# First weight pair of a spectral-mix kernel: rows of 8192 bytes, four modes per transfer and per product

## The chip, the cores and the metric

The kernel runs on one core of a Trainium2 chip. The metric is device time in microseconds (us) of one execution, all input and output transfers included. The core has TensorE (PE in the profile; PEld is its weight load), VectorE (DVE), ScalarE (ACT), GpSimd (POOL) and SyncE (SP), which here issues nearly all transfers. SBUF is the on-chip memory of 128 partitions, PSUM the memory that TensorE writes to. An engine works through its own instructions in order and waits on semaphores for the others.

## What is computed

Two stages, cut to what matters here. First, sliding-window attention with a distance bias, 8 batches, 8 heads, 576 positions, head size 64:

```python
scores = scale * np.matmul(q, k.transpose(0, 1, 3, 2))
mask = (rel >= 0) & (rel < 128)
scores = np.where(mask, scores + bias[None], -1000000000.0)
attn = softmax(scores)                       # over the last axis
x = np.matmul(attn, v)                       # -> (8, 576, 512) after the heads are joined
```

Then a mix in the spectrum along the positions, with complex weights of 512 x 512 for each of the lowest 64 modes, and a last product:

```python
X = np.fft.rfft(x, axis=1)                   # Xr, Xi: first 64 modes
Yr = np.einsum('bmd,mde->bme', Xr, w_r) - np.einsum('bmd,mde->bme', Xi, w_i)
Yi = np.einsum('bmd,mde->bme', Xr, w_i) + np.einsum('bmd,mde->bme', Xi, w_r)
y = np.fft.irfft(Y, n=S, axis=1)
u = x + y
return u + np.maximum(u @ w_ch, 0.0)
```

w_r and w_i are float32, 64 x 512 x 512 each: 134 MB together, most of what the kernel reads.

## The kernel before

**Units and pairs.** Two heads make a pair, whose outputs are 128 of the 512 columns d of x. GROUPS = ((0,), (1, 2, 3)) puts pair 0 into a first group and the other three into a second. A unit is one pair of one batch: 8 units of the first group, then 24 of the second, N = 32 in all.

**Slots.** The program is ordered by hand. `_slot(n)` writes out one step of a pipeline over the units, in this order: the first scores of unit n (PE) with their exponential (ACT, L450) and mask product (DVE, L455); the transposes of q and k of unit n+1 (PE, L411) with their copies out of PSUM (ACT, L419); the items of w0, which are products with weights; the second scores and their exponential; the casts of q, k and v to bf16 on POOL (L388, L400); the spectrum of unit n-2 (L530); the product with v of unit n-1 (L484); the mask product L460; the items of w1. An engine takes its share of this in the order written.

**Spectrum.** `_spectrum` multiplies x by a table F of cosines and sines and leaves real and imaginary part of 64 modes for the 128 columns d on 128 partitions. For the first group four batches share one PSUM tile `xt`; two DVE instructions (L540, L541) write the tile X[0], which holds -imaginary, real and imaginary part side by side. For the second group a DVE copy (L536) writes Xn, and X is made later, for eight modes at a time, by `_select`.

**Why `_select` is there.** A transfer of the second group takes, for two modes, rows of six consecutive d (12288 bytes), which puts 64 partitions of one mode and 64 of the other alternately on the 128 partitions. One product then sums over both modes' d at once, and its other operand must hold the right mode's values on each partition and zeros on the others. `_select` makes that operand on PE with selector matrices `sel`, built once by `_sel_rows` from the identity, and copies the result from PSUM with DVE (real and imaginary part) and ACT (the negative).

**Weights.** A ring of 12288 float32 per partition holds weights that wait for use. `g.parts` lists the loads: for the first group 64 parts of two modes of w_r or w_i (1024 values per partition, two rows of 2048 bytes), then 64 parts of the second (3072 values). `_load_w` issues the next part on SP as soon as the program has passed the products that use the room it needs; it is called after each `_modes`. The twelve first parts are issued among the loads of q, k and v at the start. SP's loads use eight semaphores in turn, so that each waits for the one eight before it.

**Products of the first group.** `_modes(g, 0, m0, w)` multiplies the part's weights (the upper halves of the float32 values, read as bf16) with X: for each of four blocks of 128 output columns and each of two modes a weight load and a product of 16 columns (two components x eight batches), summed in a PSUM tile `acc` for eight modes, which ACT copies to ZTa at the end. An item is two modes, w_r and w_i: 16 products. The 32 items are spread over slots 10 to 35 by the list `steps`, about one a slot and about 1.6 from slot 24 on.

**Second group.** After slot 35 the products of the second group follow with their selects, together with the work of the output as far as it is known; then `_finish`.

Of the kernel before, what the change touches and what calls it, by code (L numbers as in the profile page):

```python
# [9 lines left out]
FP32 = mybir.dt.float32  # L10
BF16 = mybir.dt.bfloat16
# [5 lines left out]
P = 128  # L17
MB = 8
# [3 lines left out]
ROWS = (1, 6)  # L22
SIZE = (1024, 3072)
# [19 lines left out]
def kernel(  # L43
# [26 lines left out]
    g.parts = [(j, m, w) for j in range(len(GROUPS)) for m in range(0, NM, 2) for w in range(2)]  # L70
# [13 lines left out]
    g.Xn = persist.tile([P, len(GROUPS[-1]), 2, B, NM], BF16)  # L84
    g.sel = persist.tile([P, 2, 2, P], BF16)
# [8 lines left out]
    with tc.manual_schedule(engines={ET.SP, ET.PE, ET.Activation, ET.DVE, ET.Pool}):  # L94
        with ExitStack() as wctx:
# [5 lines left out]
            with ExitStack() as actx:  # L101
                cp = actx.enter_context(tc.tile_pool(name="const", bufs=1))
                for j, grp in enumerate(GROUPS[:-1]):
                    g.X[j] = cp.tile([P, ROWS[j], 3, B, NM], BF16, name=f"X{j}")
# [15 lines left out]
                for n in range(n0):  # L120
                    _load_unit(g, n)
                    if n < VB - 1:
                        _load_v(g, n)
                    elif n >= VB + 2:
                        _load_v(g, n - 3)
                    if n >= g.first[1] - 1:
                        for _ in range(2):
                            _load_w(g)
# [26 lines left out]
                for j in range(len(GROUPS) - 1):  # L155
                    steps = []
                    for n in range(g.first[j + 1] + 2, g.first[j + 2] + 2):
                        steps += [n] * (SHARE if n < N - LA else SHARE_END)
                    if j + 2 == len(GROUPS):
                        steps += [n for n in range(N + 2, N + 2 + TAIL)] * SHARE_END  # L160
                    steps.sort()
                    for i, m in enumerate(range(0, NM, 2)):
                        work[steps[i * len(steps) // (NM // 2)]].append((j, m))
                _sel_rows(g)
# [25 lines left out]
            _select(g, 0)  # L190
            rest_w = [(m, w) for m in range(0, NM, 2) for w in range(2)]
            with ExitStack() as xctx:
# [4 lines left out]
                while k < len(g.seq):  # L197
# [3 lines left out]
                    if done % MB == 5 and done + 3 < NM:  # L201
                        _select(g, done + 3)
# [304 lines left out]
def _spectrum(g, n):  # L507
# [25 lines left out]
    if b % nb == nb - 1:  # L533
        b0 = b - nb + 1
        if j:
            nc.vector.tensor_copy(g.Xn[:, :, :, b], xt[:, 0])  # L536
            return
        X = g.X[j]
        xi = xt[:, :, 0].rearrange("p b i m -> p i b m")
        nc.vector.tensor_copy(X[:, 0, 1:3, b0 : b0 + nb], xi)  # L540
        nc.vector.tensor_scalar_mul(X[:, 0, 0, b0 : b0 + nb], xi[:, 1], -1.0)  # L541


def _sel_rows(g):

    nc = g.nc
    nc.vector.memset(g.sel, 0.0)
    for o in range(2):
        for h in range(2):
            nc.vector.tensor_copy(g.sel[:, o, h, h::2], g.ident_b[:, o::2])  # L550


def _select(g, m0):


    nc = g.nc
    A = len(GROUPS[-1])
    X = g.zp.tile([P, 2 * A, 3, MB, g.B], BF16, tag="Xz", bufs=2, name="Xz")
    for o in range(2):
        ps = g.fps.tile([P, g.DM], FP32, tag=("mm", "y")[o], name="xz")  # L560
        ps = ps[:, 0 : A * 2 * MB * g.B].rearrange("p (c i m b) -> p c i m b", i=2, m=MB, b=g.B)
        for h in range(2):
            nc.tensor.matmul(
                ps.rearrange("p c i m b -> p (c i) m b")[:, :, h::2], lhsT=g.sel[:, o, h],
                rhs=g.Xn.rearrange("p c i b m -> p (c i) m b")[:, :, m0 + h : m0 + MB : 2],
                start=True, stop=True)
        r = slice(A * o, A * o + A)
        nc.vector.tensor_copy(X[:, r, 1:3], ps)  # L568
        nc.scalar.mul(X[:, r, 0], ps[:, :, 1], -1.0)  # L569
    g.X[len(GROUPS) - 1, m0 // MB] = X  # L570


def _slot(g, n, w0, w1):


    N = len(g.units)
    if n < N:
        _score(g, n, 0)
# [33 lines left out]
def _places(parts):  # L612


    size = SIZE
    n0 = sum(1 for p in parts if p[0] == 0)
    at = (-n0 * size[0]) % RING
    out = []
    for j, _, _ in parts:
        if at + size[j] > RING:  # L620
            at = 0
        out.append((at, at + size[j]))
        at = (at + size[j]) % RING
    return out


def _load_w(g):
# [11 lines left out]
    src = (g.w_r, g.w_i)[w][m0 : m0 + 2, r0 : r0 + len(GROUPS[j]) * P]  # L639
# [18 lines left out]
def _pair_of_modes(g, j, m0):  # L658
    for w in range(2):
        _modes(g, j, m0, w)  # L660


def _modes(g, j, m0, w, last=False):
# [3 lines left out]
    X = g.X[j] if j == 0 else g.X[j, m0 // MB]  # L667
    A = ROWS[j]
# [7 lines left out]
    n = 2 // (SIZE[j] // (512 * A))  # L676
    for et in range(4):
        for a in range(SIZE[j] // 512):
            d, m = (a, m0) if n == 2 else (0, m0 + a)
            if j == 0:  # L680
                x = X[:, d, 1 - w : 3 - w, :, m]
            else:
                x = X[:, d, 1 - w : 3 - w, m % MB : m % MB + n]
            nc.tensor.matmul(  # L684
                acc[:, et, :, m - c0 : m - c0 + n, :],
                lhsT=wt[:, a, et * P : (et + 1) * P], rhs=x,
                start=(m0 == c0 and w == et == a == 0),
                stop=(m0 + 2 in ends and w == 1 and et == 3 and a == SIZE[j] // 512 - 1))
# [3 lines left out]
    m = m0 + 1  # L692
# [232 lines left out]
```

## Time and profile before

The time is 455.19 us, the median of three runs (452.93 to 455.75).

| | us |
|---|---|
| profiled execution, its own time | 455.69 |
| its span, first to last instruction | 453.9 |
| PE busy | 314.2 |
| DVE busy | 218.1 |
| ACT busy | 190.2 |
| POOL busy | 152.5 |
| bytes moved | 173.85 MB, 383 GB/s over the span |
| granted clock of TensorE, mean | 0.733 |

The profile is of one execution. A matmul's duration in it is longer than its share of PE, since matmuls are pipelined: where the rate matters, the distance of the starts is read. A row of a group gives, after the bar, busy time in us, mean of one in ns, and the idle time ahead of it with what ended it. A row of the chain of waits or of the timeline begins with the start and the duration in us. The share of the DMA engines can pass 1, since packets of one engine overlap.

### The profile page before, as it was taken

Reading aid. Unit: us, or ns where it says so; the run is one execution under the profiler, and the core shown is the slowest. Engines: PE = TensorE matmul, PEld = TensorE weight load, DVE = VectorE, ACT = ScalarE, POOL = GpSimd, SP = SyncE. Lnnn points to the kernel's source line nnn. Section 1 sums busy time; section 2 is a strip of 40 time slices with the busy share of each in tenths; the row PEclk is TensorE's granted clock in tenths of the full one; section 3 lists DMA queues with packets and bytes.
Section 4 is the critical chain, followed back from the end, with each engine's and each line's share of the span. In section 5 each row is a group of like instructions: output and inputs, shape, how many; then the busy total and the mean of one; then the engine's idle time right before and its main releaser. Section 6 shows DMA issues by size and latency. Waiting matters only on the chain.

```text
span 453.9 us, 12869 instructions
## 1 busy us (share of the span) xinstructions
PE 314.2 (69%) x5490; PEld 216.0 (48%) x5511; DVE 218.1 (48%) x428; ACT 190.2 (42%) x294; POOL 152.5 (34%) x262
## 2 busy tenths in 40 slices
PE   2677989988899984315656655656556766778993
PEld 2465677766778763213333333333333433554562
DVE  8468566648655451102442343434434433633683
ACT  4887666668755621001232322223222213322773
POOL 6799789779966402020000000000000000003564
PEclk9999555579755555556685786888676568998998
DMA  8999999999999999999999999999999999992687
GB/s 240 340 346 308 390 341 384 391 393 385 386 374 395 405 408 430 426 428 430 429 426 428 430 427 429 425 432 428 427 431 427 429 428 429 428 386 81 241 309 248
DMA packets 59465, 173.85 MB, mean 383 GB/s; under 512 B 4880, under 2 KB 21264, under 8 KB 51216
## 3 DMA queue, kind: packets, MB, share of 16 engines
q1 hardware_dynamic: 59024, 171.99, 96.4%
q0 software_dynamic: 384, 1.05, 1.0%
q8 instruction: 43, 0.70, 0.6%
q14 instruction: 14, 0.11, 0.1%
HBM read 163.58 MB, written 9.44 MB: 381 GB/s over the span
## 4 chain that ended last, share of the span: by engine, by line
DMA 45%; PE 34%; ACT 7%; DVE 6%; issue 4%; POOL 2%; POOLq 0%; ACTq 0%; DVEq 0%
DMA ring<-in_moe_w_r_dram 36%; DMA ring<-in_moe_w_i_dram 9%; PE acc L684 6%; PE sc L438 6%; PE xt L530 4%; PE tqk L411 4%; PE av L484 4%; ACT att L450 3%; ACT qkT L419 2%; PE mm L821 2%; PE mm L724 2%; PE y L821 1%; PE xw L737 1%; PE y L724 1%; DVE hl L743 1%
## 5 line engine op out<-in xcount | busy, mean ns | idle before, releaser
L684 PEld LDWEIGHTS <-ring 128*128 128x128 bf16 x2048 | 62.7, 103 | 122.7 <-DMA ring<-in_moe_w_i_dram 59.2
L684 PE MATMUL acc<-Xz,ring 128*128 128x32 bf16 x1536 | 51.2, 183 | 90.5 <-DMA ring<-in_moe_w_i_dram 46.1
L742 ACT CAST hl<-xw 64x512 bf16<-64x512 f32 x72 | 41.8, 580 | 125.9 <-PE xw L737 94.9
L450 ACT ACTIVATE att<-sc 128x1024 bf16<-128x1024 f32 x64 | 65.6, 1025 | 42.4 <-PE sc L438 30.5
L743 DVE TENSOR_TENSOR hl<-xw,hl 64x512 bf16<-64x512 f32 x72 | 49.6, 689 | 65.9 <-ACT hl L742 65.4
L400 POOL CAST vb<-v 64x256 bf16<-64x256 f32 x128 | 66.0, 516 | 20.7 <-PE av L484 12.8
L763 POOL MEMSET ZTa<- 32x512 bf16 x1 | 0.5, 515 | 189.2 <-ACT ZTa L760 189.2
L737 PE MATMUL xw<-wch,xT 128*128 128x512 bf16 x133 | 51.8, 524 | 3.8 <-issue 3.3
L438 PE MATMUL sc<-qkT,qkT 64*64 64x256 bf16 (+1 forms) x512 | 36.3, 365 | 19.8 <-ACT qkT L419 11.8
L419 ACT COPY qkT<-tqk 128x576 bf16<-128x576 bf16 x64 | 40.5, 634 | 0.9 <-PE tqk L411 0.9
L411 PE MATMUL tqk<-ident_b,qkb 64*64 64x64 bf16 x1152 | 35.3, 227 | 7.4 <-POOL qkb L388 7.0
L411 PEld LDWEIGHTS <-qkb 64*64 64x64 bf16 x1152 | 34.9, 142 | 10.4 <-POOL qkb L388 9.4
L484 PE MATMUL av<-vb,att 128*128 128x65 bf16 (+1 forms) x512 | 35.0, 231 | 0.9 <-DVE x L501 0.5
L455 DVE TENSOR_TENSOR att<-att,mask 128x1024 bf16<-128x1024 bf16 x32 | 28.2, 883 | 8.3 <-ACT att L450 8.2
L484 PEld LDWEIGHTS <-att 128*128 128x128 bf16 (+1 forms) x512 | 28.0, 122 | 7.6 <-issue 1.4
L717 DVE COPY xT<-tp 128x512 bf16<-128x512 bf16 x36 | 15.2, 422 | 30.3 <-PE tp L715 29.9
L737 PEld LDWEIGHTS <-xT 128*128 128x128 bf16 x144 | 17.7, 129 | 19.4 <-issue 16.1
L388 POOL CAST qkb<-q 128x576 bf16<-128x576 f32 x32 | 25.4, 793 | 4.2 <-DMA q<-in_q_dram 1.1
L388 POOL CAST qkb<-k 128x576 bf16<-128x576 f32 x32 | 26.0, 811 | 0.6 <-DMA k<-in_k_dram 0.5
L438 PEld LDWEIGHTS <-qkT 64*64 64x64 bf16 x512 | 13.4, 129 | 24.4 <-ACT qkT L419 14.2
L460 DVE TENSOR_TENSOR att<-att,mask 128x1024 bf16<-128x1024 bf16 x32 | 24.0, 749 | 1.5 <-ACT att L450 1.1
L569 ACT ACTIVATE Xz<-xz 128x192 bf16<-128x192 f32 x16 | 5.3, 331 | 41.2 <-DVE Xz L568 40.9
(110 smaller groups left out, 434.3 us busy)
## 6 DMA issues: line engine op xcount, KB each, us to landing
ring<-in_moe_w_r_dram SPq DMA_DIRECT2D x32, 1536.0 KB, 13.7
ring<-in_moe_w_i_dram SPq DMA_DIRECT2D x32, 1536.0 KB, 13.7
ring<-in_moe_w_r_dram SPq DMA_DIRECT2D x32, 512.0 KB, 7.0
ring<-in_moe_w_i_dram SPq DMA_DIRECT2D x32, 512.0 KB, 7.5
q<-in_q_dram SPq DMA_DIRECT2D x32, 288.0 KB, 6.5
k<-in_k_dram SPq DMA_DIRECT2D x32, 288.0 KB, 6.2
v<-in_v_dram SPq DMA_DIRECT2D x64, 128.0 KB, 5.8
out_dram<-o SPq DMA_DIRECT2D x32, 256.0 KB, 2.7
```

The costliest lines, as they stand in the source:

```text
L388: g.nc.gpsimd.tensor_copy(tb, t)
L400: g.nc.gpsimd.tensor_copy(o[64 * r : 64 * r + 64, i], v[64 * i : 64 * i + 64, r])
L411: g.nc.tensor.transpose(tp[hs, r, :], u.b[w][hs, r], g.ident_b[hs, hs], tile_position=(64 * hh, 64 * hh))
L419: g.nc.scalar.copy(dst.rearrange("c (p r) -> c p r", r=g.R), u.tp[w].rearrange("c r p -> c p r"))
L438: nc.tensor.matmul(sc[64 * r : 64 * r + 64, hh, 256 * i : 256 * i + nq], lhsT=kT[hs, c * P + r : c * P + P : 2], rhs=qT[hs, c * P : c * P ...
L450: nc.scalar.activation(a, sc, AF.Exp, scale=1.0 / math.sqrt(g.D))
L455: nc.vector.tensor_tensor(out=a, in0=a, in1=m, op=ALU.mult)
L484: nc.tensor.matmul(av[o, hh, col(t)], lhsT=att[c // 2][:, hh, q0 : q0 + m], rhs=u.vb[:, 2 * c + hh, 0 : D + 1], start=(j == 0), stop=(t < ...
L684: nc.tensor.matmul(acc[:, et, :, m - c0 : m - c0 + n, :], lhsT=wt[:, a, et * P : (et + 1) * P], rhs=x, start=(m0 == c0 and w == et == a == 0),
L737: nc.tensor.matmul(xw, lhsT=xT[:, dt], rhs=g.wch[:, dt], start=(dt == 0 and g.way[n] != "q"), stop=(dt == 3))
L742: nc.scalar.copy(g.hl[own, n, h], xw[own])
L743: nc.vector.tensor_tensor(out=g.hl[other, n, h], in0=xw[own], in1=g.hl[own, n, h], op=ALU.subtract)
```

## The change

JOINT = (4, 2) is the number of modes per transfer and product in each group; the first was 2 in effect before, with each mode in products of its own.

- A part of the first group is now four modes of w_r or w_i: 32 rows of 8192 bytes (four consecutive d) of each mode, on partitions that alternate among the four modes. It takes 2048 values per partition, and the ring holds six of them. There are 32 such parts, and one is issued where two were at the start.
- A product sums over all four modes and has 64 columns (two components x four modes x eight batches). An item is four modes: 32 products; there are 16 items, spread by the same list `steps`.
- The spectrum of the first group is kept in Xn[0] in the order in which it comes. `_select` now serves both groups. For the first it runs 16 small products (four offsets x four modes) into the PSUM tile that `_spectrum` uses, one DVE copy and one ACT copy. It is called at the head of slot 10 for modes 0 to 7, and for the next eight modes after every other item.
- `_sel_rows` builds a second selector of 4 x 4 matrices at the head of slot 3.

```diff
-ROWS = (1, 6)
-SIZE = (1024, 3072)
+JOINT = (4, 2)
+ROWS = (4, 6)
...
-                        for _ in range(2):
+                        for _ in range(4 // JOINT[0]):
                             _load_w(g)
...
-                    for i, m in enumerate(range(0, NM, 2)):
-                        work[steps[i * len(steps) // (NM // 2)]].append((j, m))
-                _sel_rows(g)
+                    for m in range(0, NM, JOINT[j]):
+                        work[steps[m * len(steps) // NM]].append((j, m))
+                for j in set(JOINT):
+                    _sel_rows(g, JOINT.index(j))
...
+def _sel_rows(g, j):
+    nc = g.nc
+    H = JOINT[j]
+    nc.vector.memset(g.sel[j], 0.0)
+    for o in range(H):
+        for h in range(H):
+            nc.vector.tensor_copy(g.sel[j][:, o, h, h::H], g.ident_b[:, o::H])
+
+def _select(g, j, m0):
+    nc = g.nc
+    A, H = len(GROUPS[j]), JOINT[j]
+    pool = g.zp if j else g.work
+    X = pool.tile([P, H * A, 3, MB, g.B], BF16, tag=f"Xz{j}", bufs=2, name=f"Xz{j}")
+    per = H // len(GROUPS) if j else H
+    for o0 in range(0, H, per):
         if j:
...
+            ps = g.fps.tile([P, g.DM], FP32, tag=("mm", "y")[o0], name="xz")
+        else:
+            ps = g.ps2.tile([P, g.DM], FP32, tag="xt", name="xz")
+        w = 2 * A * MB * g.B
+        for o in range(per):
+            q = ps[:, o * w : o * w + w].rearrange("p (c m b) -> p c m b", m=MB, b=g.B)
+            for h in range(H):
+                nc.tensor.matmul(
+                    q[:, :, h::H], lhsT=g.sel[j][:, o0 + o, h],
+                    rhs=g.Xn[j].rearrange("p c i b m -> p (c i) m b")[:, :, m0 + h : m0 + MB : H],
+                    start=True, stop=True)
+        q = ps[:, 0 : per * w].rearrange("p (c i m b) -> p c i m b", i=2, m=MB, b=g.B)
+        r = slice(A * o0, A * (o0 + per))
+        nc.vector.tensor_copy(X[:, r, 1:3], q)
+        nc.scalar.mul(X[:, r, 0], q[:, :, 1], -1.0)
+    g.X[j, m0 // MB] = X
...
 def _slot(g, n, w0, w1):
...
+    if n == g.first[1] + 2:
+        _select(g, 0, 0)
...
-    src = (g.w_r, g.w_i)[w][m0 : m0 + 2, r0 : r0 + len(GROUPS[j]) * P]
+    src = (g.w_r, g.w_i)[w][m0 : m0 + JOINT[j], r0 : r0 + len(GROUPS[j]) * P]
...
 def _pair_of_modes(g, j, m0):
     for w in range(2):
         _modes(g, j, m0, w)
+    if m0 % MB == MB // 2 - JOINT[j] and m0 + MB < g.NM:
+        _select(g, j, m0 // MB * MB + MB)
...
     for et in range(4):
-        for a in range(SIZE[j] // 512):
-            d, m = (a, m0) if n == 2 else (0, m0 + a)
-            if j == 0:
-                x = X[:, d, 1 - w : 3 - w, :, m]
-            else:
-                x = X[:, d, 1 - w : 3 - w, m % MB : m % MB + n]
+        for a in range(R):
             nc.tensor.matmul(
-                acc[:, et, :, m - c0 : m - c0 + n, :],
-                lhsT=wt[:, a, et * P : (et + 1) * P], rhs=x,
+                acc[:, et, :, m0 - c0 : m0 - c0 + n, :],
+                lhsT=wt[:, a, et * P : (et + 1) * P],
+                rhs=X[:, a, 1 - w : 3 - w, m0 % MB : m0 % MB + n],
```

## What I expect, and why

> **What bounds the kernel now.** I read the rate of the transfers first, then PE in stretches, then the chain of waits, then single rows. One number of the span matters throughout: the last weights land at 411.9 us, and 42 us of output work follow that the change leaves alone.
>
> The page's slices, and PE, DMA and clock by stretch (columns: us, PE, PEld, DVE, ACT, POOL busy, clock, DMA share, GB/s):
>
> ```profile
> DMA  8999999999999999999999999999999999992687
> GB/s 240 340 346 308 390 341 384 391 393 385 386 374 395 405 408 430 426 428 430 429 426 428 430 427 429 425 432 428 427 431 427 429 428 429 428 386 81 241 309 248
> ```
> ```profile
> 58.00:88.00 30.00, 28.67 (x569) 22.95 (x567) 16.92 (x37) 18.22 (x25) 25.00 (x45) 0.50 1.05 372
> 102.00:119.00 17.00, 13.81 (x417) 11.54 (x415) 14.02 (x30) 13.95 (x19) 15.68 (x26) 0.99 1.06 386
> 120.00:160.00 40.00, 38.96 (x760) 31.01 (x758) 21.31 (x48) 24.48 (x34) 24.08 (x41) 0.50 1.06 390
> ...
> 240.00:260.00 20.00, 12.29 (x153) 6.29 (x153) 6.68 (x12) 5.64 (x12) 0.00 (x0) 0.67 1.01 428
> ```
>
> The transfers never rest before 400 us. They move 428 GB/s while the second group (12288-byte rows) loads and less in the first stage, whose loads have rows of 512, 2304 and 2048 bytes. From 120 to 160 us PE is busy 39 of 40 us as well, at half clock. So the first stage has two bounds side by side. The chain of waits says the same: DMA from 166.7 us on, PE and what it waits for before.
>
> ```profile
> 163.49 0.70 DVE x_sb L498
> 164.53 0.70 DVE att L460
> 165.28 0.81 PE av L484 x9
> 166.68 9.13 DMA ring<-in_moe_w_r_dram
> 175.85 0.83 PE acc L684 x24
> 176.70 13.97 DMA ring<-in_moe_w_r_dram
> ```
>
> PE ends the first pair's products at 172.5 us, having waited 0.5 us for the last of their weights, which landed at 172.1. Transfers and PE finish the first stage together. The slack is small: when PE frees the room for the second group's first part (166.7), 5.4 us of loads are still queued.
>
> **The change, part by part.**
>
> Transfers. The first pair's 33.55 MB go from 16384 packets of 2048 bytes to 4096 of 8192. From 150 to 170 us, where hardly anything else loads, 1947 packets of 2048 bytes start in each 10 us (84 ns each, 399 GB/s): all take 84.2 us. For 8192 bytes the trace has only 18 instruction fetches: 309 ns at best, 327 in the median. The bounds: 309 ns with the overlap of the 12288-byte rows (share 1.01) gives 4096 x 309 / 16 / 1.01 = 78.4 us, 327 ns gives 83. I take 78.4, since the 12288-byte rows at 428 GB/s (78.4 us for the same bytes) agree: -5.8 us, from -1 to -5.8. As many bytes lie in the ring as before (6 parts of 1 MB for 12 of 0.5), and SP issues 32 loads fewer at about 0.4 us each, which hides under the landings it waits for.
>
> Products. Still 512 pairs of weight load and product, now 64 columns instead of 16. Single starts of the old form lie 31 ns apart (median) at either clock.
>
> ```profile
> L484 PE MATMUL av<-vb,att 128*128 128x65 bf16 x448 | 27.6, 230 | 0.9 <-DVE x L501 0.5 <-DVE att L460 0.4
> ...
> L684 PE MATMUL acc<-X,ring 128*128 128x16 bf16 x512 | 20.7, 193 | 0.5 <-DMA ring<-in_moe_w_i_dram 0.5
> ...
> L563 PE MATMUL xz<-Xn,sel 128*128 128x192 bf16 x32 | 11.6, 497 | 0.0
> ```
>
> The nearest row is the 65-column L484: 55 ns between starts at half clock, 30 at full. So +24 ns each at half clock, 12.3 us for all of them, and -0.5 us at full clock. With about a quarter of this stage at full clock, as now: +9 us.
>
> The new ordering step. Eight times 16 products of 32 columns, whose input steps through memory as in L563: there 192 columns take 325 ns from start to start at both clocks, 1.7 ns a column, so 32 take 54 ns, with the 4 that the 16-column form has above 1.7 x 16 about 58. One step is 0.93 us, all 7.4 us. From below: 30 ns each, 3.8 us. Each step also ends in a DVE copy of 512 (0.69 us, L540) and an ACT copy of 256 (about 0.4: L569 has 0.33 for 192), and ACT starts after DVE as in L569 now (40.9 us of waits on DVE). Seven steps stand ahead of the second scores: L450's second exponential, next on ACT's queue, starts 0.69 + 0.4 + 0.25 of hand-over after the step instead of 0.6 after it. That is 0.75 us late, 5 us in all, and the transposed q and k behind it on ACT (L419), which the next scores wait for, move with it. From below it is nothing, where the spectrum's matmuls cover it.
>
> Building the selector. A memset of 1024 words (272 ns for 256 now: 1.1 us) and 16 copies of 32 (0.38 us for 64: some 0.2 each) add 4.5 us on DVE at 28 us, ahead of a mask product (L455) that the next attention products wait for. Until 57 us PE waits for POOL's casts (idle 1.2 to 1.9 us in two slots), which hides most of it: +1, from 0 to +4. L540's and L541's work for the first pair falls by 0.8 us, hidden.
>
> Where the products stand. The 32 two-mode items become 16 of four modes, nearly always one a slot or none, and always before the second scores. The second half of a slot loses its product. With it PE had no idle time there (132.5 to 137.2 us), without it 0.33 us for ACT's copy; and slots that have no item become 0.3 us shorter. I set both together at -1 us, within 2.
>
> At the present clocks the sum is 9 + 7.4 + 5 + 1 - 1 = +21 us on PE: the first pair would end at 193 us.
>
> The clock. These lines are a slot at half clock (from 132.54, 4.6 us with two items) and one at full (105.35 to 108.96, 3.6 us with one):
>
> ```profile
> 134.07 0.67 PE L684 MATMUL acc<-X,ring 128*128 128x16 bf16 x16
> ...
> 135.25 1.20 PE L484 MATMUL av<-vb,att 128*128 128x65 bf16 x16
> ...
> 106.26 0.65 PE L684 MATMUL acc<-X,ring 128*128 128x16 bf16 x16
> ...
> 107.24 0.85 PE L484 MATMUL av<-vb,att 128*128 128x65 bf16 x16
> ```
>
> The clock changes in steps of 3.41 us. I summed for each step the columns that its matmuls stream, weighted by the part of the array that they use, against the 4096 that half clock allows. Half-clock steps from 58 to 160 us have 0.46 to 0.69. Up to 265 us, a half-clock step of 0.75 and more was followed by full clock in four cases of five, one of 0.62 to 0.69 in some cases and not in others. A four-mode item streams 32 x 64 full columns in 1.75 us, which takes a step of 0.57 to about 0.8. So I expect full clock for some two thirds of the stage, where it is a quarter now. All at full instead of all at half is worth 0.8 us in each of 18 slots, 1.1 in each of 8 with a spectrum (6.1 us against 4.4 + 0.6 in slot 21, which has no item) and 0.75 in each of 16 items: 35 us. Going from 1/4 to 2/3 gives back 14 to 15 us: the first pair ends at about 179 us.
>
> [...]
>
> **From there to the end.** If PE frees late, the queue runs empty: the ring's four parts of 1.5 MB (3.65 us each) then start after the item of slot 32, 6.4 us before PE's end (spectrum 2.3, wait 0.6, two items 3.5), and with 2.1 us until an empty queue delivers (an output store: 2.7 us for 256 KB) the fourth lands 10.3 us after PE's end. The other 60 parts took 225 us (187.0 to 411.9) and still will. So loads end at the later of 411.9 - 5.8 = 406.1 and PE's end + 235. PE is free to end up to 171; 177 is no change; 179 gives 414, +2 us on the profiled 455.69 (span 453.9 and 1.8 around it). The median of the runs is 455.19, half a microsecond lower; I put 458 for the change.
>
> **Rivals.**
> (a) Transfers stay the bound. Nearly all of the stage runs at full clock, or the ordering step's pieces hide; PE ends by 173. For it: at 102 to 119 us PE leaves 3 of 17 us idle. Against: it takes 22 us back. 450 to 453 us.
> (b) PE becomes the bound at the clock of now. It decides once PE ends after 181, that is with full clock in less than 0.6 of the stage. For it: steps of 0.66 and 0.69 stayed at half clock, and from 119 to 172 us nothing lifted it. PE ends at 183 to 195, 461 to 474 us.
> [...]
>
> **Chances.** My forecast (PE and transfers about even, 453 to 461 us) 0.42, (a) 0.2, (b) 0.35, (c) 0.03. A range of 450 to 470 leaves out some 0.05 of (a), 0.12 of (b) and (c). A measurement of this kernel tells about 1% (4.6 us) from no change. Faster by that needs PE's end by 172.4: the better part of (a) and a little for slots that shrink more than I count, 0.18. Slower by that begins at 459.7: (b), (c) and the upper part of my own case, 0.50. Between, 0.32.
>
> **What would show it.** 8192-byte packets near 309 ns and about 425 GB/s while they load; L684's 64-column form near 54 ns between starts at half clock, 30 at full; eight new steps of 0.9 us; the first pair's last product near 179 us; the first slices at which the DMA row falls below 9, near 165 to 180 us, if PE is the bound; the clock row above 5 at 60 to 90 and 120 to 175 us. I am wrong about the clock if that row stays at 5 (then 461 and more), and about the balance if the second group's parts still land 0.05 us ahead of their use from the first one on, with no gap in the transfers.

## The result, and the profile after

Twenty runs of each kernel gave 461.97 us (median, 457.18 to 466.06) for the change and 456.05 us (452.68 to 460.98) for the kernel before. The ratio is 1.011, with a 95% interval of 1.0085 to 1.0135: the change costs about 1%. This ratio, like all below, takes only the runs within 1.5% of their kernel's fastest; that of the two medians is 1.013. The profiled execution of the change took 457.18 us and was the fastest of its twenty, so a second profile of the same kernel (463.14 us, span 461.4; the expectations call it the second look) is read beside it.

The page's slices of the profiled execution of the change:

```profile
PEclk9987889998677897555877676667867677995998
DMA  8999999999999999999999999999999999991577
GB/s 242 371 360 294 385 345 381 387 390 370 396 351 402 422 405 412 423 429 430 428 429 428 429 428 429 429 426 430 428 428 431 430 427 424 429 382 74 211 279 277
```

The same three rows in the second profile:

```profile
PEclk9975778799987977555958676778767865897998
DMA  8999999999999989999999999999999999992578
GB/s 250 367 356 273 387 328 372 395 362 363 380 367 395 420 323 339 412 423 430 428 427 430 428 429 428 430 428 430 429 429 427 428 431 425 428 415 88 207 279 290
```

A slice of the second profile is 11.5 us. The clock row stands above 5 from the fifth slice to the sixteenth. The fifteenth and sixteenth, 161 to 185 us, are new: the DMA row falls to 8 in the fifteenth, and the rate is 323 and 339 GB/s in the two. In the kernel before, the DMA row stays at 9 from the second slice to the output, and the rate from 159 to 182 us is above 400. The first two stretches of the second profile below stand in the prediction for the kernel before (us, then PE, PEld, DVE, ACT and POOL busy, clock, DMA share, GB/s):

```profile
58.00:88.00 30.00, 23.23 (x553) 19.39 (x553) 18.24 (x36) 19.66 (x28) 24.10 (x42) 0.80 1.02 361
...
120.00:160.00 40.00, 32.29 (x814) 27.73 (x806) 24.37 (x53) 25.83 (x37) 26.86 (x46) 0.87 1.03 393
165.00:176.00 11.00, 8.90 (x164) 7.03 (x163) 7.35 (x17) 2.91 (x4) 0.00 (x0) 0.81 0.78 295
```

The third reads in the kernel before:

```profile
165.00:176.00 11.00, 7.72 (x118) 5.13 (x116) 3.40 (x11) 1.83 (x4) 2.46 (x16) 0.50 1.05 424
```

PE is busy for 32 of 40 us from 120 to 160 where it was busy for 39, at 0.87 of full clock where it had 0.50. Still it ends later, because it now waits more. From 165 to 176 us the DMA engines are busy 0.78 of the time, where they had 1.05 before. The chain of waits (start, duration, what) of the second profile says who was late:

```profile
150.73 1.04 PE acc L692 x32
151.77 0.94 PE xz L572 x16
152.73 0.70 DVE Xz L578
153.46 0.38 ACT Xz L579
153.84 0.91 ACT att L453
...
175.10 2.35 PE xt L533 x15
177.45 3.53 PE acc L692 x64
180.98 1.29 PE xz L572 x4
182.30 0.56 DVE Xz L578
182.85 0.04 DVE cvec L321
182.91 0.70 PE acc L692 x21
183.62 15.06 DMA ring<-in_moe_w_r_dram
```

PE ends the first pair's products at 181.0 us (172.6 before), and transfers become the chain only at 183.6 (166.7 before). Ahead of that the ordering step lies on the chain with all its pieces: the product, 16 small products (0.94 us), DVE's copy, ACT's copy, and only then the second exponential. The last weights land at 418.9 us (411.9 before). In the first profile PE ended at 173.3, the last weights landed at 411.8, and the transfers have no such gap: between these two executions of one kernel the stage varies by more than the change costs.

The groups that are new, in the second profile (the form of the product with 64 columns, the ordering step's products and its two copies):

```profile
L692 PE MATMUL acc<-Xz,ring 128*128 128x64 bf16 x512 | 24.3, 219 | 0.8 <-DMA v<-in_v_dram 0.7
...
L572 PE MATMUL xz<-Xn,sel 128*128 128x32 bf16 x128 | 8.7, 234 | 0.0
...
L578 DVE CAST Xz<-xz 128x512 bf16<-128x512 f32 x8 | 5.5, 690 | 3.5 <-PE xz L572 3.4
...
L579 ACT ACTIVATE Xz<-xz 128x256 bf16<-128x256 f32 x8 | 3.1, 384 | 17.2 <-DVE Xz L578 17.2
```

ACT stands idle for 17.2 us ahead of its eight new copies, 2.1 us a step, with the exponential queued behind. The 64-column products start 53 ns apart at half clock and 29 ns at full, and those of the ordering step 58 ns apart at both.

### The profile page after: what moved, and what is told of

Read it like the earlier page. It is cut to its first block, busy times and chain, and to the rows that moved or that the text cites. A ratio compares the mean times of both kernels' runs of the same rounds, so it can differ in the third digit from the quotient of the medians.

```text
span 455.4 us, 13115 instructions
## 1 busy us (share of the span) xinstructions
PE 309.3 (68%) x5639; PEld 211.5 (46%) x5639; DVE 225.2 (49%) x451; ACT 192.3 (42%) x302; POOL 153.9 (34%) x262
## 3 DMA queue, kind: packets, MB, share of 16 engines
q0 software_dynamic: 384, 1.05, 0.9%
## 4 chain that ended last, share of the span: by engine, by line
DMA 55%; PE 27%; ACT 7%; DVE 4%; issue 3%; SPq 1%; POOL 1%; POOLq 0%; ACTq 0%; DVEq 0%
DMA ring<-in_moe_w_r_dram 36%; DMA ring<-in_moe_w_i_dram 9%; PE acc L692 7%; DMA q<-in_q_dram 5%; DMA k<-in_k_dram 3%; ACT att L453 3%; PE sc L441 3%; PE xt L533 3%; ACT qkT L422 2%; PE mm L830 2%; PE xz L572 2%; PE tqk L414 2%; PE mm L733 2%; PE y L830 2%; PE av L487 2%
## 5 line engine op out<-in xcount | busy, mean ns | idle before, releaser
L692 PE MATMUL acc<-Xz,ring 128*128 128x32 bf16 (+1 forms) x2048 | 72.5, 190 | 89.8 <-DMA ring<-in_moe_w_i_dram 46.5
L746 PE MATMUL xw<-wch,xT 128*128 128x512 bf16 x144 | 55.3, 525 | 0.2 <-ACT FT L346 0.2
L441 PE MATMUL sc<-qkT,qkT 64*64 64x256 bf16 (+1 forms) x512 | 30.7, 315 | 29.8 <-ACT qkT L422 16.8
L414 PE MATMUL tqk<-ident_b,qkb 64*64 64x64 bf16 x1152 | 31.1, 213 | 8.0 <-POOL qkb L391 7.4
L414 PEld LDWEIGHTS <-qkb 64*64 64x64 bf16 x1152 | 30.8, 130 | 9.4 <-POOL qkb L391 8.0
L458 DVE TENSOR_TENSOR att<-att,mask 128x1024 bf16<-128x1024 bf16 x32 | 28.0, 876 | 13.1 <-ACT att L453 13.1
L579 ACT ACTIVATE Xz<-xz 128x192 bf16<-128x192 f32 (+1 forms) x24 | 8.4, 349 | 55.9 <-DVE Xz L578 54.8
L487 PE MATMUL av<-vb,att 128*128 128x65 bf16 (+1 forms) x512 | 29.0, 208 | 2.4 <-DVE att L463 1.9
L487 PEld LDWEIGHTS <-att 128*128 128x128 bf16 (+1 forms) x512 | 22.7, 107 | 7.9 <-DVE att L463 2.3
L578 DVE CAST Xz<-xz 128x384 bf16<-128x384 f32 (+1 forms) x24 | 14.3, 601 | 22.4 <-PE xz L572 19.7
```

Of the source, the lines that this page charges most:

```text
L414: g.nc.tensor.transpose(tp[hs, r, :], u.b[w][hs, r], g.ident_b[hs, hs], tile_position=(64 * hh, 64 * hh))
L441: nc.tensor.matmul(sc[64 * r : 64 * r + 64, hh, 256 * i : 256 * i + nq], lhsT=kT[hs, c * P + r : c * P + P : 2], rhs=qT[hs, c * P : c * P ...
L458: nc.vector.tensor_tensor(out=a, in0=a, in1=m, op=ALU.mult)
L487: nc.tensor.matmul(av[o, hh, col(t)], lhsT=att[c // 2][:, hh, q0 : q0 + m], rhs=u.vb[:, 2 * c + hh, 0 : D + 1], start=(j == 0), stop=(t < ...
L692: nc.tensor.matmul(acc[:, et, :, m0 - c0 : m0 - c0 + n, :], lhsT=wt[:, a, et * P : (et + 1) * P], rhs=X[:, a, 1 - w : 3 - w, m0 % MB : m0 ...
L746: nc.tensor.matmul(xw, lhsT=xT[:, dt], rhs=g.wch[:, dt], start=(dt == 0 and g.way[n] != "q"), stop=(dt == 3))
```

## The experiments

All times are compared with runs of the kernel before on the same chip (medians of 456.75, 455.47 and 456.0 us, one for each of three sets of runs). Ratios below 1 are faster than that kernel.

Two theories stood at first. **P**: the transfers became faster as predicted, and PE gives it all back. **T**: the transfers became no faster where attention's loads run beside them, and what PE adds is a plain loss.

**The change once more.**

> The changed kernel once more, on the chip of the other runs of this call. Theory P (PE is the late one in the first stage, and the granted clock sets how late): the first pair's last product ends between 173 and 183 us, later in an execution with less full clock between 58 and 173 us than the 0.76 of the first profile, and the last weights land about 235 to 238 us after it. Theory T (the transfers are the late ones and got no faster; the wider products are hidden): the last product ends at 172 to 174 us whatever the clock. Both: 1.008 to 1.014 of the time before.

Measured: 462.75 us, ratio 1.0099 (1.0063 to 1.0135), the profile shown above. PE ended the first pair at 181.0 us and the last weights landed 237.9 us later, as P expected; T's 172 to 174 us did not hold in this execution. The seven runs line up roughly by the clock that they were granted: 0.759 of full speed on average in the slowest (467.44 us), 0.808 in the fastest (459.84). Over the twenty runs of the result the relation is loose (a correlation of -0.35 between clock and time).

**The loads alone.** Rows, load sizes and places of the change, with the operand and the 16-column products of the kernel before and no ordering step. The weights then lie on other partitions than the products expect.

```diff
-                g.Xn[0] = cp.tile([P, 1, 2, B, NM], BF16, name="Xn0")
+                g.X0 = cp.tile([P, 1, 3, B, NM], BF16, name="X0")
...
-    if n == g.first[1] + 2:
-        _select(g, 0, 0)
...
-    if m0 % MB == MB // 2 - JOINT[j] and m0 + MB < g.NM:
-        _select(g, j, m0 // MB * MB + MB)
...
+            c, z = (m0 + a, m0 + a + 1) if j == 0 else (m0, m0 + n)
...
-                rhs=X[:, a, 1 - w : 3 - w, m0 % MB : m0 % MB + n],
+                rhs=X[:, a, 1 - w : 3 - w, c % MB : (z - 1) % MB + 1] if j else X[:, 0, 1 - w : 3 - w, :, c],
```

> The new loads (four modes, 8192-byte rows) and the new places of the items, with the spectrum, the operand and the 16-column products of before; no ordering step. The products then meet weights on other partitions than they should, so the output is not the reference's. Theory P: PE's work is that of before, PE ends the first pair by 172 us and the loads gain what the longer rows save, up to 5.8 us: 450 to 453 us, 0.987 to 0.993 of before. Theory T: the bytes moved by 100, 130 and 150 us are those of before (34.7, 46.3, 54.0 MB), 455 to 457 us, 0.997 to 1.003.

Measured: 457.9 us, ratio 1.0009 (0.9975 to 1.0043). Without PE's additions the kernel is no faster than before, which is T's value and not P's. By itself this doesn't show that the transfers gained nothing, since the products and the mean clock (0.745 against 0.743) are those of before, and PE may still bind; the kernels with fewer products, below, are the test of that.

**Short rows in the same loads.** The changed kernel, each load of 1 MB made of rows of 2048 bytes; the weights again lie on other partitions.

```diff
-        out=g.ring[:, lo:hi], in_=src.rearrange("m (p a) e -> p m (a e)", a=ROWS[j]))
+        out=g.ring[:, lo:hi], in_=src.rearrange("m (p a) e -> p m (a e)", a=ROWS[j] if j else 1))
```

> The changed kernel with each 1 MB load of the first pair made of rows of 2048 bytes (one row of each of four modes per partition), so that the weights lie on other partitions than the products expect and the output is not the reference's; all work on PE stays. Theory P: PE is late and the loads wait for it, so shorter rows cost little: 1.010 to 1.017 of before. If the longer rows are worth 5.8 us on the path, 1.022 to 1.027. Theory T: 1.008 to 1.014, and the bytes moved by 100 to 150 us are the same as with 8192-byte rows within 0.3 MB.

Measured: 459.64 us, ratio 1.0063 (1.0032 to 1.0094), below all the ranges expected, though its interval overlaps that of the change. Taking the long rows away did not make the changed kernel slower.

**Two modes instead of four.** JOINT = (2, 2) and ROWS = (2, 6): rows of 4096 bytes, loads of 0.5 MB as in the kernel before, 32-column products, and an ordering step of four products of 64 columns instead of sixteen of 32.

> The new code with two modes per transfer and product in the first group too: rows of 4096 bytes, parts of 0.5 MB, 32 two-mode items as before, products of 32 columns (27 ns apart at half clock in the second group, where the 16-column ones were 31), an ordering step of four 64-column products (about 0.11 us each by the step's 58 ns for 32 columns, 3.6 us in all for eight), no new selector. Theory P: PE at the clock of before has 3.6 - 2 + up to 5 us of late exponentials more, so it ends at 173 to 180 us, the loads gain up to 4.9 us: 452 to 459 us, 0.993 to 1.008. Theory T: 455 to 457 us, 0.998 to 1.003.

Measured: 455.38 us, ratio 0.9959 (0.9928 to 0.9991). This version beats both kernels.

The next experiments ask which part of PE's work costs the time. A further theory, **L**, came from the trace: in the changed kernel SP waits longer on its eight semaphores. From 60 to 150 us of the second profile it stood 16.0 and 7.7 us in front of loads of v until parts of w_i and w_r had landed, up to 3.0 us at a time; in the kernel before 8.4 and 4.0 us in front of loads of q and k, up to 1.1 us.

**One ordering step instead of eight.** Each eight-mode group takes the first one's operand.

```diff
-    if m0 % MB == MB // 2 - JOINT[j] and m0 + MB < g.NM:
-        _select(g, j, m0 // MB * MB + MB)
+    g.X[0, m0 // MB + 1] = g.X[0, 0]
```

> The changed kernel with only the first of its eight ordering steps; the other eight-mode groups multiply by the first one's spectrum, so the output is not the reference's. Theory P (PE decides: it ends the first pair's products at 181 us in the second look at the changed kernel, 172.6 in the kernel before, and the end follows it): seven steps of 0.93 us go, and the 0.75 us by which the second exponential was late go with them, so the first pair ends 6.5 to 11.8 us sooner, at 169 to 174.5 us, and the ratio to the kernel before is 0.996 to 1.003. Theory L (the loads of 1 MB are the cause: the small loads of the attention stand behind them, whatever PE does): the first pair ends at 178 or later, ratio 1.006 to 1.011.

Measured: 458.01 us, ratio 1.001 (0.9973 to 1.0047). The time is where P put it: with the seven ordering steps the whole loss goes, within the interval. But the first pair ended at 177.4 us in the profile, not by 174.5, and there the transfers were late, not PE: the last of the pair's weights landed only at 176.3. The stretch from 160 to 170 us, in which the second profile of the change has 0.78 of the DMA engines and 312 GB/s, reads here:

```profile
160.00:170.00 10.00, 8.27 (x205) 6.48 (x199) 6.47 (x14) 5.73 (x7) 0.75 (x1) 1.00 1.01 424
```

**Sixteen columns instead of 64.** Products of one mode each, with the ordering steps kept.

```diff
+            c, z = (m0 + a, m0 + a + 1) if j == 0 else (m0, m0 + n)
...
-                acc[:, et, :, m0 - c0 : m0 - c0 + n, :],
+                acc[:, et, :, c - c0 : z - c0, :],
...
-                rhs=X[:, a, 1 - w : 3 - w, m0 % MB : m0 % MB + n],
+                rhs=X[:, a, 1 - w : 3 - w, c % MB : (z - 1) % MB + 1],
```

> The changed kernel, but the first pair's products write one mode each (16 columns instead of 64); the other modes' columns are left out, so the output is not the reference's. Loads, places and ordering steps are those of the change. Theory P with the clock: at one clock this saves 24 ns for each of 512 products, up to 12 us, but the columns that lifted the granted clock are gone, its full share falls from two thirds to about 0.4, and the first pair ends at 183 to 188 us: ratio 1.012 to 1.025. Rival: the wide products cost PE more than the clock they bring; then it ends at 172 to 177 us, ratio 0.998 to 1.004.

Measured: 463.28 us, ratio 1.016 (1.0108 to 1.0211). In its profile PE ended the first pair at 182.5 us, just short of the range expected, and the clock was back at half for most of the stage:

```profile
PEclk9998767555557595555659677678777865897998
```

From 58 us to that end it ran at full clock for 0.23 of the time, as the kernel before (0.21), against 0.67 in the second profile of the change. That is lower than the 0.4 expected. Over all runs the mean clock was 0.738 here, 0.741 in the kernel before beside it, and 0.784 and 0.797 in the two sets of the change's runs. So the wide products bring the clock, and with it about what they cost or more; the rival, 0.998 to 1.004, falls. How much they bring on balance isn't settled: 1.016 and 1.010 have overlapping intervals. Against the run with the loads alone (1.0009), which has narrow products without the ordering steps, it is 1.5% or 6.9 us: about what ordering costs there.

**Another place for the step.** The same work as in the change; of a slot's last item the half of w_i, and the ordering step behind it, move to the slot's end.

```diff
-    for w in w0:
-        _pair_of_modes(g, *w)
+    w0, w1 = w0 + w1, []
+    for i, (j, m0) in enumerate(w0):
+        _modes(g, j, m0, 0)
+        if i + 1 < len(w0):
+            _modes(g, j, m0, 1)
+            _next_select(g, j, m0)
...
-    for w in w1:
-        _pair_of_modes(g, *w)
+    if w0:
+        j, m0 = w0[-1]
+        _modes(g, j, m0, 1)
+        _next_select(g, j, m0)
...
```

> The changed kernel, same result: of a slot's last item the real half is multiplied ahead of the second scores, as now, the imaginary half and the ordering step that may follow at the slot's end. If the ordering step's place ahead of the second exponential and the empty second half of the slot were worth what the prediction put on them (5 us and 1 us), the first pair ends at 174 to 177 us and the ratio is 0.999 to 1.003. If the place is worth nothing and only PE's amount of work counts: 181 us, 1.009 to 1.011. Theory L says 1.006 to 1.011 as well.

Measured: 456.81 us, ratio 1.0017 (0.9983 to 1.0051), and the first pair ended at 174.4 us: both as expected of the place. All the ordering steps are still there, at much the same clock (full for 0.68 of the time from 58 us to that end), and the loss is gone within the interval. So the 0.94 us a step of PE's work need not go for the loss to go; it is enough to move what stood ahead of the second scores and their exponential. The edit moves half an item along with the step, and with it ACT's copy of the sums (ZTa) after every second item; these are not told apart.

**Two modes, short rows.** The version with two modes and the line of the short rows above; the weights lie on other partitions.

> Two modes per load and per product, as in the run that gave 0.996, but with the rows of 2048 bytes of the kernel before inside the same loads of 0.5 MB (the weights then lie on other partitions than the products expect, so the output is not the reference's). If the length of the rows is worth nothing on the path: 0.993 to 0.999, as with rows of 4096 bytes. If longer rows were what made that kernel faster than the one before: 1.000 to 1.006.

Measured: 456.29 us, ratio 1.0003 (0.9973 to 1.0034). This lies at the lower end of the second expectation, but its interval overlaps the 0.9959 with longer rows. The two were not run side by side, so it decides nothing.

**The transfers with PE nearly out of the way.** One ordering step, and only the first of each part's four rows is multiplied: 128 products instead of 512. Two kernels, with long and with short rows in loads of 1 MB; they are called the light kernels.

```diff
-        for a in range(R):
+        for a in range(R if j else 1):
...
```

> The change's loads with PE's work of the first pair nearly gone: only the first of the eight ordering steps, and only the first of the four rows of each part is multiplied (128 products of 64 columns instead of 512); the rest of that sum is left out, so the output is not the reference's. PE's end of the first pair would come some 20 us sooner than in the change, so that the transfers alone set the time. If the prediction's transfer term holds (5.8 us from 8192-byte rows), the last weights land at 406 and the ratio is 0.985 to 0.990. If longer rows are worth nothing while attention's short rows load beside them: last weights at 410 to 413, ratio 0.996 to 1.002, the same as the next kernel.

> The same light kernel with rows of 2048 bytes inside the loads of 1 MB. By the prediction's transfer term it is 5.8 us slower than the one with rows of 8192 bytes, ratio 0.998 to 1.003 where that one has 0.985 to 0.990. If the length of the rows is worth nothing in the mix, the two agree within 0.3%.

Measured: 455.75 us, ratio 1.0005 (0.9971 to 1.0038) with long rows; 456.27 us, 1.0001 (0.9971 to 1.0032) with short ones. The last weights landed at 412.4 and 414.1 us. In the first, PE's last products of the pair wait 1.16 us for their weights, so the transfers do set the time. Four stretches, long rows first (the last three columns are clock, DMA share and GB/s):

```profile
80.00:100.00 20.00, 16.07 (x416) 12.83 (x410) 13.51 (x32) 15.99 (x21) 15.25 (x26) 0.91 1.00 367
100.00:120.00 20.00, 14.57 (x378) 11.69 (x371) 12.46 (x29) 14.10 (x19) 14.44 (x24) 0.79 1.03 371
...
150.00:160.00 10.00, 6.96 (x123) 5.18 (x118) 3.10 (x7) 6.26 (x9) 2.48 (x5) 0.53 1.01 425
160.00:170.00 10.00, 6.22 (x103) 4.42 (x101) 6.65 (x16) 2.63 (x3) 0.00 (x0) 0.81 1.01 423
```

The same stretches of the kernel with short rows:

```profile
80.00:100.00 20.00, 16.69 (x392) 13.21 (x391) 13.32 (x29) 15.24 (x21) 14.21 (x25) 0.83 1.05 363
100.00:120.00 20.00, 14.97 (x361) 12.07 (x361) 13.47 (x30) 13.78 (x19) 14.13 (x24) 0.77 1.00 365
...
150.00:160.00 10.00, 7.30 (x145) 5.80 (x146) 4.69 (x12) 6.14 (x9) 4.07 (x7) 0.50 1.05 406
160.00:170.00 10.00, 7.82 (x100) 5.61 (x98) 5.63 (x14) 3.40 (x5) 0.00 (x0) 0.50 1.05 407
```

From 150 us, where the first pair's weights load almost alone, long rows move 423 to 425 GB/s and short ones 406 to 407, as predicted. But only 1087 of the 4096 long packets start after 150 us. Earlier the two kernels move much the same, as far as one profile of each can tell, and both less than the kernel before (391 GB/s from 80 to 100 us, 388 from 100 to 120) or the one with two modes and short rows (391 and 390), whose loads are of 0.5 MB. The bytes moved by 150 us, which two of the expectations name, were 54.0 MB in the kernel before, 54.0 and 52.9 MB in the two profiles of the change, and 53.3 and 53.0 MB in these two kernels: in none of them more than before.

SP waits longer in that time; whether this is why the transfers move less is not shown. From 60 to 170 us, in the light kernel with long rows (us in total, times, longest; L367 loads v, L356 q and k):

```profile
SPq L367 <- DMA ring<-in_moe_w_i_dram: 15.9, 7, 3.0
...
SPq L367 <- DMA ring<-in_moe_w_r_dram: 6.6, 7, 1.8
```

In the kernel before, where L353 loads q and k:

```profile
SPq L353 <- DMA ring<-in_moe_w_i_dram: 8.4, 10, 1.1
...
SPq L353 <- DMA ring<-in_moe_w_r_dram: 4.0, 8, 0.7
```

SP stands in front of a load of 1 MB for up to 3.0 us, where it stood 1.1 in front of one of 0.5 MB. An example from the timeline (start, duration):

```profile
93.08 0.46 SPq L356 DMA_DIRECT2D k<-in_k_dram  x1
93.89 3.23 SPq L367 DMA_DIRECT2D v<-in_v_dram  x2
97.58 0.55 SPq L652 DMA_DIRECT2D ring<-in_moe_w_r_dram  x1
```

Two loads of v take 3.23 us to issue, and the weights behind them go out only at 97.6.

**Two loads where the change has one.** Each load of 1 MB is issued as two of 0.5 MB on 64 partitions each, rows of 8192 bytes kept. Other than the expectation says, this edit leaves the modes in another order on the partitions, so that its output isn't the reference's.

```diff
-    g.nc.sync.dma_start(
-        out=g.ring[:, lo:hi], in_=src.rearrange("m (p a) e -> p m (a e)", a=ROWS[j]))
+    src = src.rearrange("m (p a) e -> p m (a e)", a=ROWS[j]) if j else src
+    for i in range(1 if j else 2):
+        g.nc.sync.dma_start(
+            out=g.ring[:, lo:hi] if j else g.ring[64 * i : 64 * i + 64, lo:hi],
+            in_=src if j else src[2 * i : 2 * i + 2].rearrange("m (p a) e -> p m (a e)", a=4))
```

> The changed kernel, same result, with each load of 1 MB issued as two of 512 KB on 64 partitions each, rows still of 8192 bytes. Theory L (loads of 1 MB hold up the small loads of the attention on the eight semaphores that SP uses in turn, and so the transfers and PE): 1.000 to 1.005. Theory P (PE's ordering steps and their place are all of the loss): 1.008 to 1.012, or a little more, since SP issues 32 loads more.

Measured: 542.53 us, ratio 1.1904 (1.1857 to 1.1952). Neither theory said so. The page's rate by slices (13.5 us each):

```profile
GB/s 258 308 229 215 216 214 299 252 255 246 241 248 248 273 229 233 230 231 230 405 424 434 425 430 429 425 433 424 431 429 428 432 425 430 425 422 244 155 251 294
```

The loads of the first pair in its list of issues (count, KB each, median us from issue to landing; loads of the same size took 7.0 and 7.5 us in the kernel before):

```profile
ring<-in_moe_w_r_dram SPq DMA_DIRECT2D x32, 512.0 KB, 11.2
ring<-in_moe_w_i_dram SPq DMA_DIRECT2D x32, 512.0 KB, 13.3
```

While these loads run, up to 260 us, the rate is 214 to 308 GB/s with the DMA engines as busy as ever (a share of 1.00 from 60 to 140 us, 1.04 from 140 to 240), and a packet of 8192 bytes takes 544 to 607 ns in the means of 10 us, where it takes 309 to 311 alone in the light kernel. The experiment changed the rate of the loads, not only their number, and so says nothing of theory L, which stays open: the waits are seen, their worth was not measured by itself.

**Two modes and the other place.** The version with two modes, with the edit that moves the step.

> Two modes per load and per product (the kernel that gave 0.996) with the changed order that took the four-mode kernel from 1.010 to 1.002; same result as the reference's. If PE's order still costs that kernel time: 0.988 to 0.993. If the transfers bind it already: 0.994 to 0.998.

Measured: 454.58 us, ratio 0.9967 (0.9937 to 0.9996): as the version with two modes alone, and in the range expected if the transfers bind. In its profile PE waits for the weights of each of the last four loads of the first pair (0.35 to 0.85 us).

## Why the prediction came out as it did

It said 458 us, in a range of 450 to 470, and more likely slower than not. The time is 462: inside the range, above its own likeliest case (453 to 461), and at the low end of what rival (b) gave (461 to 474). It forecast 2.8 us more than the kernel before; by the medians it is 5.9. By its steps:

**Transfers: mis-sized.** "-5.8 us, from -1 to -5.8", of which I took the far end, is not there to be seen. The light kernels with long and short rows differ by 0.5 us in the median and 0.0004 in the ratio, with intervals of 0.003 to either side, and the light kernel's last weights landed at 412.4 us, not 406.1 (411.9 before). The price of one packet was right (309 to 311 ns alone), but I took the rate of a stretch without other loads for all 33.55 MB, and three quarters of them move beside rows of 512 and 2304 bytes. There, in the light kernel from 70 to 150 us, 8192-byte packets took 315 to 363 ns in the means of 10 us; four packets of 2048 bytes took 337 to 351 ns in the kernel before. So in the mix the long rows have hardly a gain. The lower bound of my own range (-1) was the nearer: by its profile the light kernel with long rows has its last weights 1.7 us ahead of the one with short rows, and a quarter of 5.8 us, for the quarter of the rows that load alone, would be 1.5 (an estimate). With it falls rival (a), 450 to 453 us: even with a quarter of the products and one ordering step the kernel is no faster than before, so that no clock could have brought that gain. The 458 did not suffer from this term, because it was reckoned from PE's end.

**Products: right.** 54 and 30 ns were forecast, 53 and 29 measured.

**Ordering step: right in size; in mechanism as far as shown.** 58 ns and 0.93 us a step were forecast; 58 ns and 0.94 us are measured. DVE's copy was put at 0.69 and ACT's at 0.4: 690 and 384 ns. I let the exponential start 1.34 us after the step; in the chain above it starts 1.13 us after it. That the step costs the path is shown by the run without seven of the steps, where the loss of 1.0% goes to 0.1% (-0.3 to 0.5). That its place matters is supported by the run with the steps and half an item at the slot's end, where it goes to 0.2% (-0.2 to 0.5). Neither run goes below the time of before, since the transfers are next; so the 4 us that the other place gave back are a lower bound for what the place of step and half item cost together. The 5 forecast for the late exponentials and the 1 for the empty half of the slot fit it, but no run measures the exponentials by themselves. Building the selector took 2.4 us of DVE where 4.5 was put; what it costs the path was not measured by itself either.

**Clock: right.** I said full clock for two thirds of the stage, up from a quarter. The second profile has 0.67, the first 0.76, and the kernel with narrow products falls back to 0.23. How long PE is busy does not tell the clock here: from 120 to 160 us it is busy for 32 of 40 us at 0.87 and, before, for 39 of 40 at 0.50. The prediction's own count (columns weighted by the used part of the array, in each step of 3.41 us, against 4096; the 512-column products start 427 ns apart at half clock, which comes to 4092 columns in a step) can be repeated on the profiles of the kernel before, of the change (both) and of the narrow products, from 20 to 265 us. Of 29 half-clock steps that streamed 0.75 of the 4096 columns or more, 26 were followed by full clock; of 43 that streamed less while PE was busy for 95% and more, 12 were. So the columns streamed tell much more than the busy time. That they alone decide is not shown.

**The end of the first pair: 179 forecast, 181.0 in the second profile.** The gap in the transfers came where it was announced, from 165 us on. That the figure is so near is in part luck: the first profile has 173.3 us at a clock of 0.76, and no gap.

**From there to the end: 3 us too short.** "PE's end + 235" was worked out; it measures 237.9 in the second profile, and 240.3 in the kernel with narrow products, where PE is late as well. The sum let the ring's four parts of 1.5 MB start 6.4 us before PE's end and the fourth land 10.3 us after it. In the second profile SP issued the four at these times (start, duration):

```profile
171.88 0.54 SPq L652 DMA_DIRECT2D ring<-in_moe_w_r_dram  x1
178.45 0.54 SPq L652 DMA_DIRECT2D ring<-in_moe_w_i_dram  x1
180.05 0.54 SPq L652 DMA_DIRECT2D ring<-in_moe_w_r_dram  x1
181.01 1.48 SPq L652 DMA_DIRECT2D ring<-in_moe_w_i_dram  x1
```

Only the first went out early. SP waited for the last products to free the room of the others, and issued the fourth at PE's end; it landed at 195.0 us, 14.0 after that end instead of 10.3. The other 60 parts took 224.0 us (225 forecast). 181.0 + 14.0 + 224.0 is 418.9 us, but for rounding; with the 42.4 us of output that follow and 1.8 outside the span, 463. Forecast 179 + 235 = 414 gave 458. The two differences, 2 and 3 us, are the error against this execution.

Rival (b) said that PE decides if it ends after 181, at less than 0.6 of full clock. In the second profile PE does decide, but at 0.67: the time is (b)'s, the mechanism is that of my own case, with a dearer tail. The 0.03 of (c) stood for a loss from rows 1 MiB apart; no run shows one: the light kernel with long rows, whose four modes lie so, moved 425 GB/s from 150 to 160 us, and the kernel before 403. Of the theories, T was right about the transfers, and P about PE as the late one in the second profile.

Not settled: whether the step, the half item or ACT's copy of the sums is what must not stand ahead of the exponential; why the version with two modes is 0.4% faster than before (its profile's last weights land at 412.5, no earlier); and how much of the missing transfer gain is SP's waiting behind loads of 1 MB. For the last, loads of 0.5 MB with rows of 8192 bytes would be the test, but 64 such rows fill only 64 partitions, and the run that did this lost half the rate.

## What to carry to other kernels

Price a faster transfer at the rate of the stretch in which most of its bytes move, not of the stretch where it runs alone. Before a step goes into a hand-ordered slot, look at what is queued behind its last copy on each engine; here the same step, moved to the slot's end with half an item, cost nothing measurable. A change on an engine that has only a few us of slack needs its gain elsewhere shown first, by a run in which that engine is nearly out of the way.

## What the runs showed of the hardware

Loads on 64 of the 128 partitions ran at about half the rate, although first the lower and then the upper 64 were loaded, one load behind the other: 230 to 233 GB/s in the slices from 203 to 257 us, where hardly anything else loads, against 423 to 425 in the light kernel from 150 us, with 8192-byte packets of 544 to 607 ns against 309 to 311. Why they did is not shown: the edit also changed the order in which the rows are read, and the two were not taken apart.
